# Attention maxima and sums cross the partition quadrants on VectorE instead of through a TensorE product

## Chip, cores, metric

The kernel runs on one core of one Trainium2 chip. The metric is device time in microseconds (us) of one execution, as the median of several runs.

## The reference

One transformer block with adaptive layer norm, float32 throughout. Cut to what matters here, the attention:

```python
h = _layernorm(x) * (1 + ca) + sa              # x: 2048 x 576
q = (h @ wq)                                   # 32 heads of 128
k, v = the last 512 cache rows of 16 key/value heads, each used by two query heads
scores = einsum("bhqd,bhkd->bhqk", q, k) * (128 ** -0.5)
p = softmax(scores, axis=-1)
o = einsum("bhqk,bhkd->bhqd", p, v)
x = x + ga * (o @ wo)
```

After it come a second layer norm and a gated MLP with 4608 hidden units. The softmax of one query runs over 512 keys: its maximum and its sum over the keys are what the change is about.

## The kernel before

Every float32 operand of a matmul is split into a high and a low fp32r part, and a product is made of three matmuls (high by high, low weight by high, high by low).

**Units.** The attention is cut into NU = 128 units: one head, one block of 512 queries, all 512 keys. A unit's scores lie transposed: keys on the 128 partitions, in four key tiles, and the 512 queries along the free dimension. So a maximum or a sum over the keys goes across partitions. `s_half` (twice per unit, 6 matmuls each, L495 to L497) makes the scores of two key tiles in a PSUM tile `s`.

**The maximum of a unit.** VectorE's transposing reduce (L500) takes 32x32 blocks of the scores, transposes each and reduces it: afterwards partition 32a+j holds, for key tile k and query block b, the maximum over the 32 keys of quadrant a (a quadrant is 32 partitions) for query 32b+j, in the tile `t4`, 128 x (4 x 16). `max_pre` reduces over the four key tiles (L508, into PSUM) and multiplies by a mask so that each quadrant's 16 numbers stand in a column group of their own, zero elsewhere (L509, into `t5`). `sum_pre` does the transposing reduce for the sums of the exponentials of the unit before (L515), into 16 more columns of `t5`. `spread` (L523) multiplies `t5`, 128 x 80, by the 0/1 matrix `quad`, which adds up the partitions that are equal modulo 32: every quadrant gets all four quadrants' maxima side by side, and the total of the sums. The profile shows it as two matmul records for each unit. `max_bc` then reduces the four column groups (L538), `sum_inv` takes the reciprocal of the sums (L528), and L551 transposes the maxima back into a 128x512 tile `mb`, which L568 subtracts from the scores, one half at a time. In the first four units and the last one (`by_pe`) the subtraction is a matmul instead.

**What follows in a unit.** ScalarE takes the exponential (L570) and its high part (L557), GpSimd the low part `lo` (L577, two halves). VectorE adds two of the four key tiles of exponentials (L583) and GpSimd the other two (L586) to get `ks`, which L515 reduces in the next unit. `pv_half` (L610 to L612) multiplies with the values one unit later, L533 and L618 multiply by the reciprocal sums, L622 and L626 split the result, and `wo_piece` (L637) projects pairs of units, two to four units later.

**What sets the order.** Each engine runs its instructions in the order in which the code writes them: a loop over the units writes them in steps, and at fixed times `run(u, k)` writes pieces of other work in between, from a list sorted by hand: casts and splits of weights, gates (L222), the layer norm, and towards the end preparations for the MLP (L851, L873). Within a unit PE's order is: scores (12 matmuls), query projection of the next unit (`qproj`, L423, 14), `spread`, a piece of the output projection (12 of 288 columns), the values product of the unit before (12), another output piece (12). A `psM` pool with two PSUM buffers of tag `mm` serves the query projections, the spread tiles `qm` and the value products in turn. DMAs are issued mainly from SP.

Of the kernel before, what the change touches and what calls it, by code (L numbers as in the profile page):

```python
# [7 lines left out]
F32 = mybir.dt.float32  # L8
F32R = mybir.dt.float32r
I32 = mybir.dt.int32  # L10
# [23 lines left out]
def kernel(  # L34
# [41 lines left out]

    ones = cp.tile([P, P], F32, name="ones")
    nc.vector.memset(ones, 1.0)

    ints = bp.tile([P, P], I32, tag="bc", name="ints")  # L80
    quad = cp.tile([P, P], F32, name="quad")
    nc.gpsimd.iota(ints, pattern=[[1, P]], base=P, channel_multiplier=-1)
    nc.vector.tensor_scalar(ints, ints, 31, None, op0=ALU.bitwise_and)
    nc.vector.tensor_scalar(quad, ints, 0.0, None, op0=ALU.is_equal)
    inta = bp.tile([P, 4], I32, tag="bc", name="inta")
    mask = cp.tile([P, 4], F32, name="mask")
    nc.gpsimd.iota(inta, pattern=[[-32, 4]], base=0, channel_multiplier=1)
    nc.vector.tensor_scalar(inta, inta, 5, None, op0=ALU.arith_shift_right)
    nc.vector.tensor_scalar(mask, inta, 0.0, None, op0=ALU.is_equal)

    intc = bp.tile([P, P], I32, tag="bc", name="intc")
    minus = cp.tile([P, P], F32R, name="minus")
# [386 lines left out]
        nc.vector.scalar_tensor_tensor(qlo[u], qst.pop(u)[0], SCALE, qhi[u].bitcast(F32),  # L479
                                       op0=ALU.mult, op1=ALU.subtract)  # L480

    st_, t4, t5, pt, hi_, lo_, bc, rb, rinv, ks_, pvps, done, o, bps = ({} for _ in range(14))

    def by_pe(u):
        return u < PE0 or u >= NU - PE1

    def s_half(u, h):
        g, qb, hd = unit(u)
        k = ks[g]
        t = psS.tile([P, 2, 512], F32, tag="s", name=f"s{u}_{h}")  # L490
        st_[u, h] = t
        for j in range(2):
            kt = 2 * h + j
            ps = t[:, j, :]
            nc.tensor.matmul(ps, k[:, kt, :], qhi[u], start=True, stop=False)  # L495
            nc.tensor.matmul(ps, k[:, 4 + kt, :], qhi[u], start=False, stop=False)  # L496
            nc.tensor.matmul(ps, k[:, kt, :], qlo[u], start=False, stop=True)  # L497
        if h == 0:
            t4[u] = sp.tile([P, 4, 16], F32, tag="t4", name=f"t4_{u}", bufs=1)
        nc.vector.tensor_reduce(t4[u][:, 2 * h:2 * h + 2, :].rearrange("p k b -> p (k b)"),  # L500
                                t.rearrange("p k (b j) -> p (k b) j", j=32),
                                axis=AX.X, op=ALU.max, apply_transpose=True)

    def max_pre(u):
        t5[u] = sp.tile([P, 5, 16], F32, tag="t5", name=f"t5_{u}", bufs=1)
        bps[u] = psM.tile([P, 512], F32, tag="mm", name=f"qm{u}")
        t = bps[u][:, 128:144]
        nc.vector.tensor_reduce(t, t4.pop(u).rearrange("p k b -> p b k"), axis=AX.X, op=ALU.max)  # L508
        nc.vector.tensor_tensor(t5[u][:, 0:4, :], mask[:, :, None].to_broadcast([P, 4, 16]),  # L509
                                t[:, None, :].to_broadcast([P, 4, 16]), op=ALU.mult)  # L510

    def sum_pre(u):
        if u + 1 == NU:
            t5[NU] = sp.tile([P, 5, 16], F32, tag="t5", name=f"t5_{NU}", bufs=1)
        nc.vector.tensor_reduce(t5[u + 1][:, 4, :],  # L515
                                ks_.pop(u).rearrange("p (b j) -> p b j", j=32),
                                axis=AX.X, op=ALU.add, apply_transpose=True)

    def spread(u):
        a, b = (0 if u < NU else 4), (5 if u else 4)  # L520
        if u == NU:
            bps[u] = psM.tile([P, 512], F32, tag="mm", name=f"qm{u}")
        nc.tensor.matmul(bps[u][:, a * 16:b * 16], quad,  # L523
                         t5.pop(u)[:, a:b, :].rearrange("p a b -> p (a b)"), start=True, stop=True)

    def sum_inv(u):
        r = rinv[u] = sp.tile([P, 16], F32, tag="ri", name=f"ri{u}", bufs=1)
        nc.vector.reciprocal(r, bps[u + 1][:, 64:80])  # L528

    def sum_bc(u):  # L530
        r = rinv.pop(u)
        rb[u] = bp.tile([P, 512], F32, tag="bc", name=f"rb{u}")
        nc.vector.transpose(rb[u].rearrange("p (b j) -> p b j", j=32),  # L533
                            r[:, :, None].to_broadcast([P, 16, 32]))

    def max_bc(u):
        r = bps[u][:, 256:272] if by_pe(u) else sp.tile([P, 16], F32, tag="r", name=f"r{u}", bufs=1)
        nc.vector.tensor_reduce(r, bps[u][:, :64].rearrange("p (a b) -> p b a", a=4), axis=AX.X, op=ALU.max)  # L538
# [986 lines left out]
    mlp = mlp_slots()  # L1525

    def last_unit():
        spread(NU)
        sum_inv(NU - 1)
        sum_bc(NU - 1)  # L1530
        o_mul(NU - 1)

# [80 lines left out]
    for u in range(NU):  # L1613
# [114 lines left out]
```

## Time and profile before

| | |
|---|---|
| median of 3 runs | 2887.05 us (2883.12 to 2887.52) |
| the profiled execution | 2884.48 us, its span 2882.7 us |
| granted TensorE clock, mean | 0.997 |
| attention units | from 35 to 1634 us of the span |
| MLP | from 1634 us to the end |

"Busy" is the time in which an engine runs at least one instruction. A row of a timeline view gives start, length, engine, line, operation, tiles, shapes and count; in square brackets stands how long the engine was idle before it and who ended that. A row of the groups view gives the count, then busy time and mean duration in ns, then the engine's idle time ahead of the group.

### The profile page before, as it was taken

What the parts mean: (1) busy time and instruction counts of PE and PEld (TensorE: products, weight loads), DVE (VectorE), ACT (ScalarE), POOL (GpSimd) and SP (SyncE); (2) the same over time, 40 slices, a digit from 0 to 9 for tenths busy, and PEclk for the clock granted to TensorE, in tenths of its full rate; (3) what the DMA queues carried; (4) which work ended last, traced back from release to release, by engine and by line L of the source; (5) the groups of instructions that cost most, each with busy time, mean ns of one, the idle gap of its engine ahead of it and who ended that gap; (6) DMA issues with size and microseconds to landing.
All of it is one profiled execution on the core that took longest, in us unless ns stands there. A gap on an engine that the chain in (4) does not pass through costs nothing.

```text
span 2882.7 us, 41271 instructions
## 1 busy us (share of the span) xinstructions
PE 2839.4 (98%) x15214; PEld 2476.9 (86%) x15214; DVE 2149.1 (75%) x2967; ACT 1496.2 (52%) x2105; POOL 2115.0 (73%) x1564
## 2 busy tenths in 40 slices
PE   6999999999999999999999999999999999999999
PEld 5788888888888888888888888888888888888888
DVE  7778788888878888777889756676677466666666
ACT  5666666666676666666656444444444222222221
POOL 5688888888888889776778666787787356656553
PEclk9999999999999999999999999999999999999999
DMA  4012222222223223322244456666667944444442
GB/s 161 23 46 70 72 101 83 71 90 99 97 83 100 92 64 135 103 71 87 66 131 145 149 216 218 233 243 232 228 228 256 354 160 156 154 154 155 160 153 106
DMA packets 164362, 399.59 MB, mean 139 GB/s; under 512 B 15040, under 2 KB 61888, under 8 KB 164160
## 3 DMA queue, kind: packets, MB, share of 16 engines
q1 hardware_dynamic: 132912, 284.84, 30.1%
q10 hardware_dynamic: 31248, 112.11, 9.9%
q8 instruction: 121, 1.98, 0.3%
q14 instruction: 81, 0.66, 0.1%
HBM read 271.16 MB, written 154.57 MB: 148 GB/s over the span
## 4 chain that ended last, share of the span: by engine, by line
PE 90%; POOL 3%; DVE 2%; ACT 2%; DMA 2%; issue 1%; SPq 0%; ACTq 0%; POOLq 0%; DVEq 0%
PE gu L981 26%; PE wo L637 13%; PE qps L423 13%; PE md L637 8%; PE st_P L1083 6%; PE s L497 4%; PE s L496 4%; PE s L495 4%; PE pv L612 4%; PE pv L611 4%; PE pv L610 4%; PE qm L523 1%; POOL lo L577 1%; ACT p L570 0%; DVE ws L788 0%
## 5 line engine op out<-in xcount | busy, mean ns | idle before, releaser
L577 POOL TENSOR_TENSOR lo<-p,hi 128x1024 fp32r<-128x1024 f32 x256 | 608.7, 2399 | 1.1 <-ACT hi L557 1.1
L586 POOL TENSOR_TENSOR ks<-ks,p 128x512 f32<-128x512 f32 x256 | 343.8, 1343 | 270.6 <-ACT p L570 212.6
L500 DVE TRANSPOSE_TENSOR_REDUCE t<-s 128x32 f32<-128x1024 f32 x256 | 316.6, 1244 | 136.9 <-PE s L497 125.6
L981 PE MATMUL gu<-hop_B,wop 128*128 128x512 f32 x1512 | 374.5, 391 | 0.2 <-DMA wop<-wk_P 0.2
L981 PEld LDWEIGHTS gu<-hop_B,wop 128*128 128x128 f32 x1512 | 275.0, 188 | 50.5 <-ACT lflh L966 0.9
L981 PE MATMUL gu<-hop_T,wop 128*128 128x512 f32 x1260 | 316.0, 391 | 0.0
L423 PE MATMUL qps<-hTa,wA 128*128 128x512 f32 x1288 | 311.4, 392 | 4.2 <-DVE hTa L371 2.1
L637 PE MATMUL wo<-woga,ohi 128*128 128x288 f32 x1472 | 306.5, 301 | 0.0
L568 DVE TENSOR_TENSOR p<-s,mb 128x1024 f32<-128x1024 f32 x246 | 290.2, 1218 | 4.1
L423 PEld LDWEIGHTS qps<-hTa,wA 128*128 128x128 f32 x1288 | 242.8, 189 | 57.4 <-DVE hTa L371 4.2
L557 ACT CAST hi<-p 128x1024 fp32r<-128x1024 f32 x256 | 269.1, 1051 | 7.1
L570 ACT ACTIVATE p<-p 128x1024 f32<-128x1024 f32 x246 | 259.8, 1056 | 7.6 <-DVE p L568 7.3
L637 PE MATMUL md<-wogb,hhi 128*128 128x288 f32 x1280 | 258.9, 295 | 3.6 <-DVE acc L648 2.6
L981 PEld LDWEIGHTS gu<-hop_T,wop 128*128 128x128 f32 x1260 | 227.8, 188 | 38.9
L475 ACT ACTIVATE qhi<-qps 128x512 fp32r<-128x512 f32 x128 | 76.5, 597 | 340.4 <-PE qps L423 340.4
L637 PEld LDWEIGHTS wo<-woga,ohi 128*128 128x128 f32 x1472 | 239.2, 189 | 7.3
L648 DVE TENSOR_TENSOR acc<-md,acc 128x576 f32<-128x576 f32 x160 | 120.7, 755 | 160.8 <-PE md L637 160.3
L637 PEld LDWEIGHTS md<-wogb,hhi 128*128 128x128 f32 x1280 | 212.2, 188 | 16.6 <-DVE acc L648 4.3
L637 PE MATMUL wo<-woga,olo 128*128 128x288 f32 x736 | 217.4, 295 | 0.3 <-POOL olo L626 0.2
L1092 DVE TENSOR_TENSOR acc<-st_P,acc 128x576 f32<-128x576 f32 x160 | 121.0, 757 | 128.0 <-PE st_P L1083 128.0
L637 PE MATMUL md<-wogb,hlo 128*128 128x288 f32 x640 | 188.6, 295 | 0.0
L646 ACT COPY acc<-wo 128x576 f32<-128x576 f32 x233 | 148.2, 636 | 66.8 <-PE wo L637 60.4
(274 smaller groups left out, 7107.2 us busy)
## 6 DMA issues: line engine op xcount, KB each, us to landing
wop<-wk_P SPq DMA_DIRECT2D x133, 640.0 KB
wk_P<-wop ACTq DMA_DIRECT2D x119, 640.0 KB
wr<-wlay SPq DMA_DIRECT2D x68, 384.0 KB
rogb<-wd SPq DMA_DIRECT2D x68, 288.0 KB
againq<-akq SPq DMA_DIRECT2D x18, 640.0 KB
rwA<-wq SPq DMA_DIRECT2D x32, 320.0 KB
wlay<-wg SPq DMA_DIRECT2D x36, 256.0 KB
roga<-wo SPq DMA_DIRECT2D x32, 288.0 KB
```

The source lines that it names most:

```text
L423: return [lambda i=i, a=a, b=b: nc.tensor.matmul(ps, a, b, start=(i == 0), stop=(i == n - 1)) for i, (a, b) in enumerate(ops)]
L500: nc.vector.tensor_reduce(t4[u][:, 2 * h:2 * h + 2, :].rearrange("p k b -> p (k b)"), t.rearrange("p k (b j) -> p (k b) j", j=32), axis=AX ...
L557: nc.scalar.copy(hi_[u, h], pt[u, h])
L568: nc.vector.tensor_tensor(p, t, bc[u][:, None, :].to_broadcast([P, 2, 512]), op=ALU.subtract)
L570: nc.scalar.activation(p, p, AF.Exp, bias=0.0, scale=1.0)
L577: nc.gpsimd.tensor_sub(lo_[u, h], pt[u, h], hi_[u, h].bitcast(F32))
L586: nc.gpsimd.tensor_tensor(ks_[u], ks_[u], p[:, j, :], op=ALU.add)
L637: nc.tensor.matmul(ps[:, half, :H2], a[:, sl], w[b][:, cs], start=(n == 0 and seed is None), stop=(n == 5), skip_group_check=seed is not None)
L646: nc.scalar.copy(av, ps[:, :, :H2])
L981: nc.tensor.matmul(ps, a, c, start=s not in heir(m) and i == 0 and s not in seeds_of(m), stop=i == len(ops) - 1, skip_group_check=True)
L1083: nc.tensor.matmul(ps[:, j, :H2], x[:, sl], w[:, y, :], start=n == 0 and not second, stop=n == 2, skip_group_check=True)
L1092: nc.vector.tensor_tensor(t, ps[:, :, :H2], t, op=ALU.add)
```

## The change

The maxima and sums no longer go through PE. The tile `t5` becomes 128 x 21 rows of 16 numbers. The transposing reduces write row 0 of a group of four rows for each key tile and for the sums; `cross` then moves with VectorE instructions whose output partitions differ from their input partitions (`move`: a reduce over an axis of length one). First partitions 64 to 127 to partitions 0 to 63 (5 x 16 numbers), then 32 to 63 to 0 to 31 (5 x 2 x 16). Then quadrant 0 holds everything: one reduce of 16 rows gives the maxima (256 numbers in), one of 4 rows gives the sums (64 in), and two more moves (32 numbers each) copy both to quadrant 1 and then to quadrants 2 and 3. `max_pre`, `spread` and `sum_inv` go, with the matrix `quad`, the mask and the PSUM tile `qm`; the reciprocal is taken in `sum_bc`. `max_bc` stands before the next unit's query projection in the code, where it stood behind it.

```diff
-        nc.vector.tensor_reduce(t4[u][:, 2 * h:2 * h + 2, :].rearrange("p k b -> p (k b)"),
+        nc.vector.tensor_reduce(t5[u][:, 8 * h:8 * h + 8:4, :],
                                 t.rearrange("p k (b j) -> p (k b) j", j=32),
                                 axis=AX.X, op=ALU.max, apply_transpose=True)
-    def max_pre(u):
-        t5[u] = sp.tile([P, 5, 16], F32, tag="t5", name=f"t5_{u}", bufs=1)
-        bps[u] = psM.tile([P, 512], F32, tag="mm", name=f"qm{u}")
-        t = bps[u][:, 128:144]
-        nc.vector.tensor_reduce(t, t4.pop(u).rearrange("p k b -> p b k"), axis=AX.X, op=ALU.max)
-        nc.vector.tensor_tensor(t5[u][:, 0:4, :], mask[:, :, None].to_broadcast([P, 4, 16]),
-                                t[:, None, :].to_broadcast([P, 4, 16]), op=ALU.mult)
-
-    def spread(u):
...
-        nc.tensor.matmul(bps[u][:, a * 16:b * 16], quad,
-                         t5.pop(u)[:, a:b, :].rearrange("p a b -> p (a b)"), start=True, stop=True)
-
-    def sum_inv(u):
-        r = rinv[u] = sp.tile([P, 16], F32, tag="ri", name=f"ri{u}", bufs=1)
-        nc.vector.reciprocal(r, bps[u + 1][:, 64:80])
+    def move(dst, src):
+        nc.vector.tensor_reduce(dst, src[..., None], axis=AX.X, op=ALU.max)
+
+    def cross(u):
+        t = t5.pop(u)
+        v = t[:, 0:20, :].rearrange("p (k a) b -> p k a b", a=4)[:, (0 if u < NU else 4):(5 if u else 4)]
+        move(v[0:64, :, 1, :], v[64:128, :, 0, :])
+        move(v[0:32, :, 2:4, :], v[32:64, :, 0:2, :])
+        r = rr_[u] = t[:, 15:21:5, :]
+        if u < NU:
+            nc.vector.tensor_reduce(r[0:32, 1, :], t[0:32, 0:16, :].rearrange("p n b -> p b n"), axis=AX.X, op=ALU.max)
+        if u:
+            nc.vector.tensor_reduce(r[0:32, 0, :], t[0:32, 16:20, :].rearrange("p n b -> p b n"), axis=AX.X, op=ALU.add)
+        w = slice(0 if u else 1, 2 if u < NU else 1)
+        move(r[32:64, w, :], r[0:32, w, :])
+        move(r[64:128, w, :], r[0:64, w, :])
 
     def sum_bc(u):
-        r = rinv.pop(u)
+        r = rr_.pop(u + 1)[:, 0, :]
+        nc.vector.reciprocal(r, r)
         rb[u] = bp.tile([P, 512], F32, tag="bc", name=f"rb{u}")
...
     def max_bc(u):
-        r = bps[u][:, 256:272] if by_pe(u) else sp.tile([P, 16], F32, tag="r", name=f"r{u}", bufs=1)
-        nc.vector.tensor_reduce(r, bps[u][:, :64].rearrange("p (a b) -> p b a", a=4), axis=AX.X, op=ALU.max)
-        if u:
-            sum_inv(u - 1)
+        r = rr_[u][:, 1, :]
...
         s_half(u, 0)
         s_half(u, 1)
         run(u, .5)
-        max_pre(u)
         if u:
             sum_pre(u - 1)
+        cross(u)
+        max_bc(u)
         run(u, 1)
         if u + 1 < NU:
             qproj(u + 1, 0, 14)
...
         run(u, 2)
-        spread(u)
-        max_bc(u)
         if u + 1 < NU:
             q_hi(u + 1)
```

VectorE's instructions in a middle unit (unit 78), from behind the two score reduces, before the change:

```order
L508 TENSOR_REDUCE qm_10576<-t_78_10565 128x16
L509 TENSOR_TENSOR t_78_10575<-mask,qm_10576 128x64
L515 TENSOR_REDUCE t_78_10575<-ks_10512 128x16
L538 TENSOR_REDUCE r_10596<-qm_10576 128x16
L528 RECIPROCAL ri_10598<-qm_10576 128x16
L551 STREAM_TRANSPOSE mb_10600<-r_10596 128x512
L568 TENSOR_TENSOR p_0_10633<-s_0_10558,mb_10600 128x1024
L568 TENSOR_TENSOR p_1_10638<-s_1_10567,mb_10600 128x1024
L533 STREAM_TRANSPOSE rb_10641<-ri_10598 128x512
```

And in the changed kernel, the next unit, at the same place (its line numbers are smaller; L501 is `move`, L510 and L512 the two reduces of `cross`, L536 the transpose of the maxima, L519 the reciprocal):

```order
L496 TENSOR_REDUCE t_79_10526<-ks_10481 128x16
L501 TENSOR_REDUCE t_79_10526<-t_79_10526 64x5x16
L501 TENSOR_REDUCE t_79_10526<-t_79_10526 32x5x32
L510 TENSOR_REDUCE t_79_10526<-t_79_10526 32x16
L512 TENSOR_REDUCE t_79_10526<-t_79_10526 32x16
L501 TENSOR_REDUCE t_79_10526<-t_79_10526 32x2x16
L501 TENSOR_REDUCE t_79_10526<-t_79_10526 64x2x16
L536 STREAM_TRANSPOSE mb_10543<-t_79_10526 128x512
L553 TENSOR_TENSOR p_0_10589<-s_0_10519,mb_10543 128x1024
L553 TENSOR_TENSOR p_1_10594<-s_1_10528,mb_10543 128x1024
L519 RECIPROCAL t_79_10526<-t_79_10526 128x16
L521 STREAM_TRANSPOSE rb_10598<-t_79_10526 128x512
```

Three instructions (L508, L509, L538) went, six came, and the reciprocal moved behind the two subtractions. Each of the six waits for the one ahead of it.

PE at the end of a query projection in unit 78, before the change (`qps` is the projection, `wo` an output piece):

```order
L423 MATMUL qps_10580<-hTa_6_1254,wA_9625 128x512
L423 MATMUL qps_10580<-hTa_7_1256,wA_9625 128x512
L523 MATMUL qm_10576<-t_78_10575,quad 128x80
L637 MATMUL wo_1_10544<-woga_9911,ohi_10298 128x288 x2
L637 MATMUL wo_1_10544<-woga_9911,olo_10300 128x288
```

And in the changed kernel, one unit later:

```order
L412 MATMUL qps_10545<-hTa_6_533,wA_10260 128x512
L412 MATMUL qps_10545<-hTa_7_535,wA_10260 128x512
L622 MATMUL wo_3_10511<-woga_9759,ohi_10140 128x288 x2
L622 MATMUL wo_3_10511<-woga_9759,olo_10142 128x288
L622 MATMUL wo_3_10511<-woga_10071,ohi_10323 128x288 x2
```

The product with `quad` is gone and PE goes from the projection straight to the output piece.

More of the change, by code (lines that the diff above doesn't have):

```diff
@@ L78 @@
     nc.vector.memset(ones, 1.0)
[L80 to L89, printed above, removed]
     intc = bp.tile([P, P], I32, tag="bc", name="intc")
@@ L480, in q_lo @@
                                        op0=ALU.mult, op1=ALU.subtract)
-    st_, t4, t5, pt, hi_, lo_, bc, rb, rinv, ks_, pvps, done, o, bps = ({} for _ in range(14))
+    st_, t5, pt, hi_, lo_, bc, rb, rr_, ks_, pvps, done, o = ({} for _ in range(12))
     def by_pe(u):
@@ L498, in s_half @@
         if h == 0:
-            t4[u] = sp.tile([P, 4, 16], F32, tag="t4", name=f"t4_{u}", bufs=1)
-        nc.vector.tensor_reduce(t4[u][:, 2 * h:2 * h + 2, :].rearrange("p k b -> p (k b)"),
+            t5[u] = sp.tile([P, 21, 16], F32, tag="t5", name=f"t5_{u}", bufs=1)
+        nc.vector.tensor_reduce(t5[u][:, 8 * h:8 * h + 8:4, :],
                                 t.rearrange("p k (b j) -> p (k b) j", j=32),
                                 axis=AX.X, op=ALU.max, apply_transpose=True)
-    def max_pre(u):
-        t5[u] = sp.tile([P, 5, 16], F32, tag="t5", name=f"t5_{u}", bufs=1)
-        bps[u] = psM.tile([P, 512], F32, tag="mm", name=f"qm{u}")
-        t = bps[u][:, 128:144]
-        nc.vector.tensor_reduce(t, t4.pop(u).rearrange("p k b -> p b k"), axis=AX.X, op=ALU.max)
-        nc.vector.tensor_tensor(t5[u][:, 0:4, :], mask[:, :, None].to_broadcast([P, 4, 16]),
-                                t[:, None, :].to_broadcast([P, 4, 16]), op=ALU.mult)
@@ L512, in sum_pre @@
     def sum_pre(u):
         if u + 1 == NU:
-            t5[NU] = sp.tile([P, 5, 16], F32, tag="t5", name=f"t5_{NU}", bufs=1)
-        nc.vector.tensor_reduce(t5[u + 1][:, 4, :],
+            t5[NU] = sp.tile([P, 21, 16], F32, tag="t5", name=f"t5_{NU}", bufs=1)
+        nc.vector.tensor_reduce(t5[u + 1][:, 16, :],
                                 ks_.pop(u).rearrange("p (b j) -> p b j", j=32),
                                 axis=AX.X, op=ALU.add, apply_transpose=True)
-    def spread(u):
[L520 to L523, printed above, removed]
-                         t5.pop(u)[:, a:b, :].rearrange("p a b -> p (a b)"), start=True, stop=True)
@@ L1527, in last_unit @@
     def last_unit():
-        spread(NU)
-        sum_inv(NU - 1)
+        cross(NU)
         sum_bc(NU - 1)
```

## The prediction, made before the changed kernel ran

> **What bounds the kernel now.** First the page: busy times, and the chain of work that ended last.
>
> ```profile
> PE 2839.4 (98%) x15214; PEld 2476.9 (86%) x15214; DVE 2149.1 (75%) x2967; ACT 1496.2 (52%) x2105; POOL 2115.0 (73%) x1564
> PE 90%; POOL 3%; DVE 2%; ACT 2%; DMA 2%; issue 1%; SPq 0%; ACTq 0%; POOLq 0%; DVEq 0%
> ```
>
> PE is the bound, and DVE's 75% is a mean over the attention and an MLP that the change doesn't touch. So I read a middle unit in the timeline: DVE's rows from one unit's scores to the next, and PE's rows around the two places where an output piece follows a 512-column product.
>
> ```profile
> 1005.13 2.61 DVE L500 TRANSPOSE_TENSOR_REDUCE t<-s 128x32 f32<-128x1024 f32 x2 [1.60 <-PE s L497]
> ...
> 1006.29 3.34 PE L423 MATMUL qps<-hTa,wA 128*128 128x512 f32 x14
> ...
> 1007.77 0.27 DVE L508 TENSOR_REDUCE qm<-t 128x16 f32<-128x64 f32 x1
> 1008.08 0.22 DVE L509 TENSOR_TENSOR t<-mask,qm 128x64 f32<-128x64 f32 x1
> 1008.22 0.70 DVE L515 TRANSPOSE_TENSOR_REDUCE t<-ks 128x16 f32<-128x512 f32 x1
> ...
> 1009.47 0.35 PE L523 MATMUL qm<-t,quad 128*128 128x80 f32 x2
> ...
> 1009.85 0.23 DVE L538 TENSOR_REDUCE r<-qm 128x16 f32<-128x64 f32 x1 [0.93 <-PE qm L523]
> ...
> 1010.00 0.25 DVE L528 RECIPROCAL ri<-qm 128x16 f32<-128x16 f32 x1
> ...
> 1010.16 0.67 DVE L551 STREAM_TRANSPOSE mb<-r 128x512 f32<-128x512 f32 x1
> ...
> 1011.30 0.39 PE L610 MATMUL pv<-hi,kv 128*128 128x512 f32 x1
> ...
> 1013.13 0.70 DVE L533 STREAM_TRANSPOSE rb<-ri 128x512 f32<-128x512 f32 x1
> ...
> 1013.76 0.65 DVE L479 SCALAR_TENSOR_TENSOR qlo<-qps,qhi 128x512 fp32r<-128x512 f32 x1
> ...
> 1013.82 0.39 PE L612 MATMUL pv<-lo,kv 128*128 128x512 f32 x1
> ...
> 1015.63 0.39 PE L495 MATMUL s<-qhi,kv 128*128 128x512 f32 x1
> ...
> 1016.08 0.40 PE L497 MATMUL s<-qlo,kv 128*128 128x512 f32 x1
> ...
> 1017.21 2.61 DVE L500 TRANSPOSE_TENSOR_REDUCE t<-s 128x32 f32<-128x1024 f32 x2 [1.17 <-PE s L497]
> ```
>
> The unit takes 1017.21 - 1005.13 = 12.08 us. PE has no gap; DVE waits twice, 0.93 us for `qm` and 1.17 us for scores. How much of such waiting there is shows in the groups of L500 and L538, asked for four stretches: units 0 to 5 (35 to 130 us), 6 to 108 (to 1380), ten units beside the second layer norm (to 1510), the last eight (to 1604).
>
> ```profile
> L500 DVE TRANSPOSE_TENSOR_REDUCE t<-s 128x32 f32<-128x1024 f32 x14 | 17.0, 1235 | 2.4 <-PE s L497 2.1
> ...
> L538 DVE TENSOR_REDUCE qm<-qm 128x16 f32<-128x64 f32 x4 | 0.9, 233 | 3.3 <-PE qm L523 3.3
> ...
> L538 DVE TENSOR_REDUCE r<-qm 128x16 f32<-128x64 f32 x2 | 0.4, 224 | 1.5 <-PE qm L523 1.5
> ```
> ```profile
> L500 DVE TRANSPOSE_TENSOR_REDUCE t<-s 128x32 f32<-128x1024 f32 x205 | 254.8, 1246 | 128.8 <-PE s L497 118.6
> L538 DVE TENSOR_REDUCE r<-qm 128x16 f32<-128x64 f32 x103 | 23.1, 224 | 91.9 <-PE qm L523 91.9
> ```
> ```profile
> L500 DVE TRANSPOSE_TENSOR_REDUCE t<-s 128x32 f32<-128x1024 f32 x22 | 27.0, 1238 | 4.7 <-PE s L497 3.9
> L538 DVE TENSOR_REDUCE r<-qm 128x16 f32<-128x64 f32 x10 | 2.2, 225 | 10.7 <-PE qm L523 10.7
> ```
> ```profile
> L500 DVE TRANSPOSE_TENSOR_REDUCE t<-s 128x32 f32<-128x1024 f32 x15 | 17.9, 1221 | 1.1 <-PE s L497 1.0
> L538 DVE TENSOR_REDUCE r<-qm 128x16 f32<-128x64 f32 x8 | 1.8, 224 | 4.9 <-PE qm L523 4.9
> ```
>
> DVE's free time is 118.6 + 91.9 = 210.5 us in the long stretch, 2.0 us for each unit, but 14.6 us in the next ten units and 5.9 us in the last eight (0.7 each). There DVE is as full as PE.
>
> **What goes on PE.** After the projection's last product (end 1006.29 + 3.34 = 1009.63) with `qm` and twelve output matmuls behind it, the next product starts at 1011.30, 1.67 us later; after L612 (end 1014.21), with twelve output matmuls alone, at 1015.63, 1.42 us later. The product with `quad` thus costs PE 0.25 us per unit, although its two records last 0.35. A unit bounded by PE goes from 12.08 to 11.83 us.
>
> **What comes on DVE.** The score reduce takes 1.246 us for 1024 numbers and L515 0.70 for 512: 1.07 ns for each and 0.16 fixed. L538 (64 numbers, from PSUM, 0.224) fits that. The two first moves (80 and 160 numbers a partition) would take 0.24 and 0.33, the last two (32 each) 0.19 each. The reduces over rows step 16 numbers at every read, as L508 does, and L508, with L538's shape, takes 0.27: 0.05 more. So the sum reduce (64 numbers) takes 0.23 to 0.28, the maximum (256) 0.43, or, if the 0.05 grows with the count, 0.63. The six together, X, take 1.61 to 1.86. I take 1.85, for the step is the only difference between L508 and L538 besides which memory they read and write. [...]
>
> No row shows an output in another quadrant than its input. From below this costs nothing, since half the partitions or all take the same time where the shapes are alike. From above I allow each of the four moves one more fixed part, 0.16: X = 2.5. I take nothing extra. [...]
>
> Each of the six, and L551, waits for the one ahead; such hand-overs take 0.03 us (L508 ends at 1008.04, L509 starts at 1008.08). From the end of the score reduces (1007.74) to L551 the DVE's own time was 1010.16 - 1007.74 - 0.93 = 1.49 us. Now it is L515 (0.70, overlapping by 0.08 what is ahead, as it does behind L509: end 1008.30, start 1008.22), X, and seven hand-overs (0.24): 0.86 + X = 2.71. So L551 starts 0.29 later after the scores than before, though it waits for nothing on PE. The reciprocal now stands before L533, 0.25 + 0.03 on its own. DVE's load per unit grows by 2.71 - 1.49 + 0.28 = **1.5 us** (1.26 at X = 1.61, 2.15 at X = 2.5).
>
> **What is late next.** `qlo` for the next unit (L479) ended at 1014.41, PE's first use is at 1016.08: 1.67 us of slack, of which 0.29 + 0.28 + 0.25 go. 0.85 is left: a plain unit is fine, and one late by less than that too. The tighter path is the GpSimd one: scores, L551, exponential, `ks`, then `lo`, which PE needs in the next unit. Where GpSimd also splits a query weight ahead of it, it reads:
>
> ```profile
> 1018.62 1.56 POOL L182 TENSOR_TENSOR wA<-rwA,wA 128x640 fp32r<-128x640 f32 x1
> 1020.14 4.76 POOL L577 TENSOR_TENSOR lo<-p,hi 128x1024 fp32r<-128x1024 f32 x2
> ```
> ```profile
> 1025.22 0.39 PE L612 MATMUL pv<-lo,kv 128*128 128x512 f32 x1
> ```
> ```profile
> L182 POOL TENSOR_TENSOR wA<-rwA,wA 128x640 fp32r<-128x640 f32 x29 | 45.7, 1575 | 0.0
> ```
>
> The second half of `lo` ends at 1024.90, PE wants it at 1025.22: 0.32 us. Two `quad` products lie between, so PE arrives 0.50 earlier, and `lo` ends 0.29 later: PE waits 0.47. There are 29 such splits in the long stretch; in 22 units, counted in the timeline, `lo` ends within 0.45 us of its use, most at 0.32 or 0.33. 22 x 0.47 = 10.3 us.
>
> **The sum**, against the profiled execution (2884.48 us, 2.6 below the median of the runs).
> - Long stretch: 103 x 0.25 = 25.8 us gained; 10.3 go back to `lo`. DVE's 210.5 us free pay for 103 x 1.5 = 155 and the 25.8, but L500 waited for scores 89 times only (the row below, from L500 asked alone in this stretch): 14 of the 103 units began with no wait, for gates and other work on DVE. They become 12.08 - 0.93 + 1.5 = 12.65 us of DVE, 0.8 more than PE's 11.83. The slack covers `qlo`, not `lo`; I charge 0.5 each, 7 us. Net 8.5 gained.
>
> ```profile
>   PE s L497: 118.6, 89
> ```
>
> - Next ten units: 10 x 1.5 = 15 us against 14.6 free: nothing gained.
> - Last eight units: 12 against 5.9; 6.1 us longer, less the 0.85 that `qlo` covers: 5 lost.
> - First six: PE isn't the bound there; 6 x 1.5 = 9 on DVE against 2.1 plus 4.8 us of waits: 2 lost.
> - PE's own waits for what DVE put into `qm` go, 3.2 us:
>
> ```profile
> PE qm L523 <- DVE t L515: 3.2, 4, 1.5
> ```
>
> 8.5 - 5 - 2 + 3.2 = 4.7 us gained, 0.16%: 2879.8 on the profiled execution, 2882.4 on the median. A part of DVE's load that I can't count, dependent instructions that start late in units that are late already, speaks for a little more, and I take **2884**. With X from 1.61 to 2.0 (0.1 us of X moves the sum by about 4 us: 22 times on `lo`, 14 + 8 + 6 times on DVE) the sum goes from 14 gained to 1 lost; charging the 14 uneven units their whole 0.8 and as much again for those behind them takes it to 10 lost. On the median the case is 2873 to 2897. As cover: the product that goes was PE time in full, and what comes is hidden behind PE only where DVE waited.
>
> **The rivals.**
> 1. *Nearly the whole gain.* The six cost at most 1.3 us, say because handed-over small instructions overlap more than their records show. Then 0.95 comes per unit, L551 starts 0.26 earlier than now, `lo`'s deficit shrinks to nothing, the last eight lose 1.7: 25.8 + 3.2 - 1.7 - 2 and up to 7 for uneven units, 18 to 25 gained: 2862 to 2873 with the edge of the forecast. For it: 2.0 us of free DVE time per unit in the long stretch. Against it: L538, the shortest reduce in the rows above, takes 0.22, and six of those are 1.3.
> 2. *DVE becomes the bound* (the other side). If the moves cost a fixed part more, X = 2.5 and 2.15 come per unit: 221 us in the long stretch against 210.5 - 25.8 free. It decides from (210.5 - 25.8) / 103 = 1.8 per unit, X = 2.15. At 2.15: 11 longer there by mean load, some 5 for unevenness, 7 in the next ten, 11 in the last eight, 6 in the first, and 3.2 back: 37 longer. At X = 2.2 the 4 us per 0.1 give some 10. 2898 to 2925. For it: the last eight units already have no room, as this one shows:
>
> ```profile
> 1549.38 0.22 DVE L538 TENSOR_REDUCE r<-qm 128x16 f32<-128x64 f32 x1 [0.54 <-PE qm L523]
> ...
> 1555.65 1.78 DVE L851 TENSOR_TENSOR h<-h,h 128x512 f32<-128x512 f32 x1
> 1557.35 2.37 DVE L500 TRANSPOSE_TENSOR_REDUCE t<-s 128x32 f32<-128x1024 f32 x2
> ```
>
> DVE there starts the scores late, with 0.54 us free in a whole unit, and a 512-number sum takes 1.78 instead of the 0.70 of L515's 512. If later starts bring more of these long ones, the price rises too. Against it: nothing shows that a move costs more than its numbers.
> 3. *It doesn't do what it says.* PE would gain nothing if weight loads and not products set its pace there. The two 1.67 and 1.42 us stretches speak against it. Without the 25.8, and with `lo` late by almost nothing, the 5, the 2 and a little for uneven units stay: 5 to 8 us longer, 2892 to 2895. [...]
>
> **How the numbers follow.** The forecast case (2873 to 2897) has a chance of 0.53, rival 1 0.20, rival 2 0.25, rival 3 0.02. About 0.2% (5.8 us) is what a measurement of this kernel can tell from no change. Of the forecast case 0.15 lies below 2881.3, 0.22 between, 0.16 above 2892.8. Faster: 0.20 + 0.15 = 0.35; the same 0.22; slower 0.25 + 0.16 + 0.02 = 0.43. The range reaches into both rivals, 2864 to 2913.
>
> **What would show it.** In the changed profile: (a) no L523, and plain units of 11.83 us; (b) the six at 0.24, 0.33, 0.63, 0.28, 0.19, 0.19 us; the maximum reduce is the one I know least; (c) the wait before L500 down from 1.17 to about 0.3 to 0.4 in plain units, no other wait ahead of the transpose; (d) waits of PE for `lo`, 22 or more, near 0.5 us each; (e) the last eight units longer than before, some by 0.7 us. The prediction is wrong if X is under 1.3 or over 2.1, if PE waits for `qlo` in the long stretch, or if the MLP's time moves.

## The result and the profile after

The changed kernel takes 2897.34 us (median of 6 runs, 2896.66 to 2899.86), the kernel before 2886.45 us (6 runs, 2883.12 to 2887.71). The ratio is 1.0043, with a 95% interval of 1.0033 to 1.0052: 0.4% slower, where a gain of about 0.1% was forecast. The profiled execution has a span of 2894.9 us (2882.7 before), 12.2 longer.

The page of the changed kernel, busy times and the chain that ended last:

```profile
PE 2825.1 (98%) x14956; PEld 2443.7 (84%) x14956; DVE 2302.0 (80%) x3351; ACT 1498.9 (52%) x2105; POOL 2125.3 (73%) x1562
PE 64%; DVE 10%; POOL 5%; issue 3%; ACT 2%; DMA 2%; ACTq 0%; POOLq 0%; SPq 0%; DVEq 0%
```

PE is busy for 14.3 us less, yet its part of the chain fell from 90% to 64% and DVE's rose from 2% to 10%. A middle unit of the changed kernel, DVE's rows from one unit's scores to the next:

```profile
1253.81 2.61 DVE L489 TRANSPOSE_TENSOR_REDUCE t<-s 128x32 f32<-128x1024 f32 x2 [0.87 <-PE s L486]
1256.34 0.67 DVE L496 TRANSPOSE_TENSOR_REDUCE t<-ks 128x16 f32<-128x512 f32 x1
1257.04 0.57 DVE L501 TENSOR_REDUCE t<-t 64x80 f32<-64x80 f32 x2
1257.65 0.59 DVE L510 TENSOR_REDUCE t<-t 32x16 f32<-32x256 f32 x1
1258.27 0.25 DVE L512 TENSOR_REDUCE t<-t 32x16 f32<-32x64 f32 x1
1258.56 0.39 DVE L501 TENSOR_REDUCE t<-t 32x32 f32<-32x32 f32 x2
1258.98 0.71 DVE L536 STREAM_TRANSPOSE mb<-t 128x512 f32<-128x512 f32 x1
...
1265.63 1.25 DVE L489 TRANSPOSE_TENSOR_REDUCE t<-s 128x32 f32<-128x1024 f32 x1 [0.87 <-PE s L486]
```

The unit takes 1265.63 - 1253.81 = 11.82 us, and the only wait left is the one for scores. So the plain unit went from 12.08 to 11.83 as forecast; 48 of the 103 units from 6 to 108 take this, from first score to first score. The durations of the six, and the waits for scores, over units 6 to 108 (groups, forms apart, 127 to 1372 us):

```profile
L489 DVE TRANSPOSE_TENSOR_REDUCE t<-s 128x32 f32<-128x1024 f32 x206 | 253.1, 1240 | 63.1 <-PE s L486 55.1
L510 DVE TENSOR_REDUCE t<-t 32x16 f32<-32x256 f32 x103 | 60.7, 589 | 3.6
```

The first two moves take 0.231 and 0.307 us, the sum reduce 0.253, the last two moves 0.176 and 0.180; with 0.589 for the maximum, X is 1.74 (1.85 was taken).

Where the time went shows when the span is cut at the first score product of units 0, 6, 109, 119 and 127 and at the first `gu` product of the MLP (all from the timelines; us; the kernels below the second row are the experiments):

| kernel | units 0-5 | 6-108 | 109-118 | 119-126 | last unit to MLP | MLP to the end |
|---|---|---|---|---|---|---|
| before | 91.1 | 1253.5 | 126.6 | 97.1 | 11.7 | 1267.3 |
| changed | 91.9 | 1244.5 | 132.5 | 104.3 | 17.8 | 1268.4 |
| late_ten | 91.9 | 1244.3 | 126.4 | 104.4 | 17.8 | 1270.6 |
| last9_pe | 92.5 | 1243.8 | 132.6 | 97.2 | 11.7 | 1273.7 |
| last1_pe | 92.6 | 1243.3 | 132.5 | 104.3 | 15.5 | 1270.8 |
| from109_pe | 91.8 | 1244.1 | 126.6 | 97.0 | 11.7 | 1274.2 |
| no_cross | 86.5 | 1232.6 | 123.5 | 95.5 | 12.4 | 1270.5 |
| max2 | 94.3 | 1272.4 | 140.8 | 109.3 | 18.3 | 1267.5 |
| pre | 90.0 | 1237.7 | 129.0 | 101.0 | 16.4 | 1267.8 |
| pre_from109_pe | 90.2 | 1237.3 | 126.3 | 97.1 | 11.7 | 1275.3 |
| pre_late_ten | 90.5 | 1237.4 | 124.5 | 101.0 | 17.0 | 1267.5 |
| pre_late_ten_last9 | 90.9 | 1237.4 | 124.6 | 97.0 | 11.7 | 1268.5 |
| warm | 92.0 | 1244.8 | 132.6 | 104.3 | 16.1 | 1271.0 |

From the first row to the second the attention changes by +0.8, -9.0, +5.9, +7.2 and +6.1 us, and the MLP by +1.1. The long stretch gained nearly what the prediction said; the three places behind it took back 19.2 us.

**The ten units.** DVE and PE in one of the four units where the layer norm's affine step stands (L340 before, L329 now). First before the change, DVE's rows, then PE's output piece behind the product with `quad`:

```profile
1447.17 0.70 DVE L515 TRANSPOSE_TENSOR_REDUCE t<-ks 128x16 f32<-128x512 f32 x1
1447.80 0.77 DVE L340 TENSOR_SCALAR lfb<-ltb,mcol,mcol 128x512 f32<-128x512 f32 x1
1449.69 0.22 DVE L538 TENSOR_REDUCE r<-qm 128x16 f32<-128x64 f32 x1 [1.12 <-PE qm L523]
```
```profile
1449.31 0.35 PE L523 MATMUL qm<-t,quad 128*128 128x80 f32 x2
1449.45 0.52 PE L637 MATMUL wo<-againo,ohi 128*128 128x288 f32 x2
```

The same place in the changed kernel, and who waited for L329 in units 109 to 118:

```profile
1443.33 0.39 DVE L501 TENSOR_REDUCE t<-t 32x32 f32<-32x32 f32 x2
1443.76 0.71 DVE L536 STREAM_TRANSPOSE mb<-t 128x512 f32<-128x512 f32 x1
1444.39 0.77 DVE L329 TENSOR_SCALAR lfb<-ltb,mcol,mcol 128x512 f32<-128x512 f32 x1
```
```profile
1445.21 0.54 PE L622 MATMUL wo<-againo,ohi 128*128 128x288 f32 x2 [1.23 <-DVE lfb L329]
```
```profile
  PE wo L622: 5.0, 4
```

Before, L340 ran inside the wait for `qm`, which cost nothing. Now the code writes it behind the whole crossing and the transpose. It reads a PSUM tile of the pool `psW`, and the next output piece needs that buffer: PE stands still for 1.23 us, four times, 5.0 us.

**The last unit.** It has no next projection that covers its maxima. Windows of the changed kernel from its first score product on (columns: stretch, its length, busy time and count of each engine, granted clock of TensorE, share and rate of DMA):

```profile
1608.70:1617.40 8.70, 6.82 (x34) 4.98 (x33) 8.67 (x11) 4.90 (x6) 5.77 (x4) 1.00 0.30 90
1617.40:1622.00 4.60, 1.71 (x6) 0.83 (x6) 3.74 (x12) 0.91 (x2) 2.26 (x1) 0.88 0.53 174
1622.00:1626.50 4.50, 4.50 (x16) 4.11 (x17) 1.74 (x3) 4.12 (x6) 1.60 (x2) 0.50 0.05 15
1626.50:1630.00 3.50, 3.50 (x18) 3.05 (x18) 0.76 (x1) 1.20 (x2) 3.42 (x3) 0.82 0.00 0
```

And its DVE rows:

```profile
1613.32 1.77 DVE L836 TENSOR_TENSOR h<-h,h 128x512 f32<-128x512 f32 x1
1615.01 2.37 DVE L489 TRANSPOSE_TENSOR_REDUCE t<-s 128x32 f32<-128x1024 f32 x2
...
1620.34 0.71 DVE L531 STREAM_TRANSPOSE mb<-rr 128x512 f32<-128x512 f32 x1
```

DVE is busy without a break (8.67 of 8.70 us) and reaches the last scores at 1615.01, behind a backlog of the units ahead; the maxima come at 1620.34. PE runs for only 1.71 of the 4.60 us up to 1622, and then its granted clock is 0.50 for 4.5 us and 0.82 on the mean of another 3.5. At the same place before the change the four subtractions came 8.8 us after the first score product (1612.47), PE was busy for 3.27 of 4.40 us, and the clock stayed at 1.00:

```profile
1608.00:1612.40 4.40, 3.27 (x16) 2.25 (x14) 2.81 (x9) 0.60 (x2) 3.83 (x2) 1.00 0.77 264
1612.40:1616.00 3.60, 3.60 (x20) 2.92 (x20) 2.27 (x4) 3.57 (x6) 1.29 (x1) 1.00 0.38 112
```

The four subtractions, before and with the change:

```profile
1612.47 1.20 PE L564 MATMUL s<-mr,minus 128*128 128x512 f32 x4
```
```profile
1621.76 2.07 PE L549 MATMUL s<-mr,minus 128*128 128x512 f32 x4 [1.31 <-ACT mr L534]
```

They start 13.1 us after the unit's first score product (1608.7) instead of 8.8, which is 4.3 of the 6.1 us. From their start to the first `gu` product it is 4.75 us instead of 2.94, with no wait in between: 1.8 us for the low clock.

### The profile page after: what moved, and what is told of

It is laid out like the page before. It is cut to its first block, busy times and chain, and to the rows that moved or that the text cites. A ratio compares the mean times of both kernels' runs of the same rounds, so it can differ in the third digit from the quotient of the medians.

```text
span 2894.9 us, 41010 instructions
## 1 busy us (share of the span) xinstructions
PE 2825.1 (98%) x14956; PEld 2443.7 (84%) x14956; DVE 2302.0 (80%) x3351; ACT 1498.9 (52%) x2105; POOL 2125.3 (73%) x1562
## 4 chain that ended last, share of the span: by engine, by line
PE 64%; DVE 10%; POOL 5%; issue 3%; ACT 2%; DMA 2%; ACTq 0%; POOLq 0%; SPq 0%; DVEq 0%
PE gu L966 24%; PE wo L622 7%; PE md L622 7%; PE qps L412 7%; PE st_P L1068 6%; PE s L486 2%; PE s L485 2%; PE s L484 2%; PE pv L597 2%; DVE t L489 2%; PE pv L596 2%; PE pv L595 2%; POOL lo L562 2%; DVE p L553 1%; DVE t L501 1%
## 5 line engine op out<-in xcount | busy, mean ns | idle before, releaser
L571 POOL TENSOR_TENSOR ks<-ks,p 128x512 f32<-128x512 f32 x256 | 349.8, 1366 | 268.1 <-ACT p L555 168.0
L489 DVE TRANSPOSE_TENSOR_REDUCE t<-s 128x32 f32<-128x1024 f32 x256 | 313.2, 1237 | 67.7 <-PE s L486 58.7
L622 PE MATMUL wo<-woga,ohi 128*128 128x288 f32 x1472 | 299.8, 295 | 2.3 <-POOL woga L171 1.4
L622 PEld LDWEIGHTS wo<-woga,ohi 128*128 128x128 f32 x1472 | 246.2, 188 | 19.6 <-POOL woga L171 4.3
L966 PE MATMUL gu<-hy_T,wop 128*128 128x512 f32 x540 | 174.7, 392 | 0.5 <-POOL wop L745 0.5
```

The lines of the kernel that those rows point to most:

```text
L489: nc.vector.tensor_reduce(t5[u][:, 8 * h:8 * h + 8:4, :], t.rearrange("p k (b j) -> p (k b) j", j=32), axis=AX.X, op=ALU.max, apply_transp ...
L571: nc.gpsimd.tensor_tensor(ks_[u], ks_[u], p[:, j, :], op=ALU.add)
L622: nc.tensor.matmul(ps[:, half, :H2], a[:, sl], w[b][:, cs], start=(n == 0 and seed is None), stop=(n == 5), skip_group_check=seed is not None)
L966: nc.tensor.matmul(ps, a, c, start=s not in heir(m) and i == 0 and s not in seeds_of(m), stop=i == len(ops) - 1, skip_group_check=True)
```

## The experiments

Three theories stood at the start. *Order*: the ten units lose because L329 moved behind the crossing. *Backlog*: the last eight units push DVE behind, and the last unit pays for it, with the lowered clock on top. *Load*, the rival to both: DVE has 1.4 us more per unit, and where it stands doesn't matter. All times are medians; ratios are to the kernel before, run on the same chip (17 to 26 runs of it beside the first eight, 9 beside the last three).

### late_ten: the crossing behind the inserted work, units 109 to 118

```diff
             sum_pre(u - 1)
-        cross(u)
-        max_bc(u)
+        if not (109 <= u < 119):
+            cross(u)
+            max_bc(u)
         run(u, 1)
...
         run(u, 2)
+        if 109 <= u < 119:
+            cross(u)
+            max_bc(u)
```

> The changed kernel, with the crossing and the transpose of the maxima written behind the inserted work (after run(u, 2)) in units 109 to 118 only. Order theory: the ten units lost 5.9 us because the affine step of the layer norm (L329, about 1.25 us), which stood in the wait for qm before the change, now stands behind the crossing, so that the output pieces wait for their PSUM buffer. Then units 109 to 118 take 126.6 to 128 us from first score to first score instead of 132.5, and the run is 4 to 6 us faster than the changed kernel (2891 to 2893). Load theory: DVE has 1.5 us more work per unit in ten units that had 14.6 us free, and its place doesn't matter: 131.5 to 133.5 us, no change of the run (2896 to 2898). Both expect the last nine units to stay as they are in the changed kernel.

2892.6 us, ratio 1.0022 (1.0013 to 1.0031). Units 109 to 118 take 126.4 us instead of 132.5, and the last nine units are as in the changed kernel. DVE's rows of the same unit:

```profile
1439.35 0.67 DVE L496 TRANSPOSE_TENSOR_REDUCE t<-ks 128x16 f32<-128x512 f32 x1
1439.94 0.77 DVE L329 TENSOR_SCALAR lfb<-ltb,mcol,mcol 128x512 f32<-128x512 f32 x1
1440.74 0.57 DVE L501 TENSOR_REDUCE t<-t 64x80 f32<-64x80 f32 x2
```

L329, which takes 0.77 us and not the 1.25 expected, is back behind the sum reduce, and nobody waits for it. The work on DVE is the same to the instruction, so load alone is not the cause there: order is.

### last9_pe, last1_pe, from109_pe: the TensorE product back from a unit on

`old(u)` is `u >= 119`, `u >= 127` or `u >= 109`; for those units `max_pre`, `spread` and `sum_inv` are those of before, on rows of the same tile, with `quad` brought by a DMA into the tile of ones that is no longer needed.

```diff
+        if old(u):
+            max_pre(u)
         if u:
             sum_pre(u - 1)
-        cross(u)
-        max_bc(u)
+        if not old(u):
+            cross(u)
+            max_bc(u)
...
         run(u, 2)
+        if old(u):
+            spread(u)
+            max_bc(u)
```

> The changed kernel, with the TensorE product of before in units 119 to 127 and for the last sums (quad comes back by a DMA into the tile of ones, three units ahead). Backlog theory: the eight units let DVE fall behind, and the last unit inherits that, whose late maxima leave PE idle for about 4 us, after which its clock is halved. Then all of it comes back: 5.6 us in units 119 to 125, 1.5 in unit 126, 6 between the last scores and the first product of the MLP, 1.6 at the low clock; 13 to 15 us faster than the changed kernel, 2882 to 2885. Own-chain theory: the six instructions in the last unit are themselves the longer chain; then the same comes back here, and only the next run tells them apart.

2885.8 us, ratio 1.0005 (0.9997 to 1.0014), 11.5 us faster than the changed kernel, a little less than the 13 to 15 expected. Units 119 to 126 and the last unit go back to 97.2 and 11.7 us, their times before the change.

> The changed kernel, with the TensorE product of before in the last unit and for the last sums only. Backlog theory: the last unit's scores still find DVE behind by about 3 us, so at most 2 to 3 us come back, 2894 to 2897, and PE is still idle for 3 us or more ahead of the subtraction of the maxima, with a clock of 0.5 behind it. Own-chain theory: 6 to 8 us come back, 2889 to 2891, PE idle for under 2 us there and at full clock behind it.

2896.72 us, ratio 1.0038 (1.0024 to 1.0052): at most a microsecond. The last unit takes 15.5 us instead of 17.8. DVE still comes late:

```profile
1616.14 2.37 DVE L505 TRANSPOSE_TENSOR_REDUCE t<-s 128x32 f32<-128x1024 f32 x2
```

L505 starts 6.3 us after the unit's first score product (1609.8), L489 in the changed kernel 6.3 after it (1608.7), L500 before 2.2 after it (1605.92 against 1603.7). Of the 6.1 us that the last unit lost, 3.8 remain with the old chain (15.5 against 11.7): the backlog. The other 2.3 are not all the unit's own chain. The subtractions start here 12.6 us after the first score product, 0.5 sooner than the 13.1 of the changed kernel, and that is what the chain costs:

```profile
1622.44 1.20 PE L591 MATMUL s<-mr,minus 128*128 128x512 f32 x4 [0.87 <-ACT mr L576]
```

The rest, 1.8 us, is the low clock, which this run doesn't have. That was expected wrongly: the clock stayed at 1.00, with PE busy for 2.87 us of the same 4.60 and not for 1.71.

```profile
1617.40:1622.00 4.60, 2.87 (x12) 1.45 (x10) 3.63 (x9) 0.23 (x1) 3.39 (x2) 1.00 0.59 170
1622.00:1626.50 4.50, 4.05 (x21) 3.35 (x22) 2.67 (x4) 4.44 (x7) 1.33 (x2) 1.00 0.24 83
```

> The changed kernel in units 0 to 108, and the TensorE product of before from unit 109 on. If the three places add up as the positions in the two traces say, this keeps the 9 us gained by unit 109 and loses nothing behind it: 2876 to 2879, a ratio to the kernel before of 0.9965 to 0.9975. If the gain up to unit 109 is given back anywhere else (the MLP, the end of the attention), 2883 to 2888.

2881.31 us, ratio 0.9988 (0.9979 to 0.9997): 4 us faster than before, not 8 or 9. At the first `gu` product this kernel is 8.2 us ahead of before (1607.2 against 1615.4), as the three places add up. In its profile the MLP then takes 1274.2 us instead of 1267.3. What PE waited for there:

```profile
PE md L664 <- DVE acc L675: 6.2, 3, 3.6
```

The longest of these three, 3.6 us, stands behind a sum on DVE that took 7.27 us where its like takes 0.94 (last section). Over all profiles here the MLP takes 1267 to 1275 us, and its code is the same in all. The profile of `pre_from109_pe` below has the same wait of 3.6 us behind a sum of 7.30 and the longest MLP; no other profile has a sum on DVE over 6.1 us there. But the two profiled executions are 2.2 and 5.3 us above the medians of their kernels, so they may not stand for all runs. Whether the kernels that arrive at some times have the long MLP more often, or by chance, stays open.

### no_cross and max2: the price of the chain from both sides

```diff
     def cross(u):
-        t = t5.pop(u)
...
+        rr_[u] = t5.pop(u)[:, 12:17:4, :]
```
```diff
         if u < NU:
+            nc.vector.tensor_reduce(r[32:64, 1, :], t[0:32, 0:16, :].rearrange("p n b -> p b n"), axis=AX.X, op=ALU.max)
             nc.vector.tensor_reduce(r[0:32, 1, :], t[0:32, 0:16, :].rearrange("p n b -> p b n"), axis=AX.X, op=ALU.max)
```

> The changed kernel without the six crossing instructions: nothing crosses the quadrants, and the transposes read one row of the uncrossed maxima and sums. It leaves that part of the computation out, so its time is that of TensorE's gain alone. DVE theory (every loss of the changed kernel is DVE being late; TensorE would have gained 0.25 us in every unit): units 6 to 108 take 1226 to 1229 us from first score to first score (1253.5 before, 1244.5 with the change), the last eight 12.0 or less each, and PE is at full clock behind the last unit; 28 to 33 us faster than the kernel before, 2852 to 2857. Rival, PE theory (the uneven units are late for reasons on PE and GpSimd that have nothing to do with the six): the long stretch stays at 1235 us or more, 2862 or slower.

2857.18 us, ratio 0.9903 (0.9890 to 0.9915), 28.6 us faster than before. The long stretch takes 1232.6 us, between the two theories: TensorE's gain is there (it was 1253.5), but 14 us over 103 x 11.83 stay. The weight loads of PE waited for this (127 to 1372 us in the changed kernel, then 122 to 1355 us without the crossing):

```profile
PEld pv L597 <- POOL lo L562: 10.4, 23, 1.1
PEld wo L622 <- POOL olo L611: 5.5, 11, 0.8
PEld s L486 <- DVE qlo L468: 4.5, 5, 1.7
```
```profile
PEld pv L586 <- POOL lo L551: 7.3, 21, 1.1
PEld wo L611 <- POOL olo L600: 2.8, 4, 1.2
```

Of the 10.4 us for `lo`, 7.3 are there without a crossing, most of them as waits of 0.25 us: PE comes 0.25 us earlier with each product that goes, and the low part doesn't come earlier with the maxima. In one such unit the first half of the subtraction is done at some 990.8 us, but ScalarE takes its exponential only at 993.15, behind two copies of an output piece for which it had waited 1.04 us. The crossing's own part is the rest and the waits for `qlo`. So this run prices the product and the crossing together, and not the product alone: DVE has 0.4 us less per unit in it than in the kernel before (9.48 against 9.88 us busy in units 6 to 108).

> The changed kernel with the reduce of the maxima written twice, its first result into a place that is overwritten: 0.59 us more and a hand-over, 0.62 per unit, in the chain of DVE. The prediction's slope of 4 us for 0.1 us gives 25 us more, 2919 to 2925. Bound theory (DVE is now the bound, so a unit grows by all that is added): 126 x 0.62 = 78 us more, 2970 to 2976. Slack theory (plain units have 0.9 us of slack ahead of qlo, so they stay at 11.83 and only the units that are uneven already grow): 15 to 35 us more, with plain units of 11.83 to 11.9 still there.

2942.15 us, ratio 1.0199 (1.0186 to 1.0212): 45 us more than the changed kernel for 0.62 us per unit, 7.2 us for each 0.1. Not the 78 of a kernel bound by DVE throughout, and more than the 35 of the slack theory. In the long stretch it is 27.9 us (4.5 for 0.1), and 34 of its 103 units still take 11.8 (48 in the changed kernel); units 109 to 118 add 8.3, units 119 to 126 add 5.0. PE's loads wait for `qlo` 29 times now:

```profile
PEld pv L598 <- POOL lo L563: 20.1, 28, 1.1
PEld s L486 <- DVE qlo L468: 16.5, 29, 2.3
```

### pre: key tiles reduced first

All 128 partitions reduce their own four key tiles (as L508 did before the change), so that one row crosses and not four.

```diff
+        if u < NU:
+            nc.vector.tensor_reduce(t[:, 0, :], t[:, 10:14, :].rearrange("p n b -> p b n"), axis=AX.X, op=ALU.max)
-        v = t[:, 0:20, :].rearrange("p (k a) b -> p k a b", a=4)[:, (0 if u < NU else 4):(5 if u else 4)]
+        v = t[:, 0:8, :].rearrange("p (k a) b -> p k a b", a=4)[:, (0 if u < NU else 1):(2 if u else 1)]
...
-            nc.vector.tensor_reduce(r[0:32, 1, :], t[0:32, 0:16, :].rearrange("p n b -> p b n"), axis=AX.X, op=ALU.max)
+            nc.vector.tensor_reduce(r[0:32, 1, :], t[0:32, 0:4, :].rearrange("p n b -> p b n"), axis=AX.X, op=ALU.max)
```

> The changed kernel, the key tiles reduced first on all 128 partitions (64 numbers), so that the moves and the second reduce carry a quarter of the numbers: seven instructions of about 0.25, 0.18, 0.23, 0.25, 0.25, 0.18 and 0.18 us, 1.52 us against 1.74, and one hand-over more, 0.18 us less per unit. By the slope of 4 us for 0.1 us 7 us faster than the changed kernel, 2889 to 2891. If the number of handed-over instructions is what costs and not their length, no faster than the changed kernel, 2896 to 2899.

2883.35 us, ratio 0.9991 (0.9983 to 1.0000), 14 us faster than the changed kernel, twice what was expected. Its groups over units 6 to 108:

```profile
L501 DVE TENSOR_REDUCE t<-t 64x32 f32<-64x32 f32 x206 | 37.2, 180 | 7.1
L512 DVE TENSOR_REDUCE t<-t 32x16 f32<-32x64 f32 x103 | 26.2, 255 | 3.6
L514 DVE TENSOR_REDUCE t<-t 32x16 f32<-32x64 f32 x103 | 25.1, 244 | 0.0
L506 DVE TENSOR_REDUCE t<-t 128x16 f32<-128x64 f32 x103 | 23.0, 223 | 0.0
L501 DVE TENSOR_REDUCE t<-t 32x64 f32<-32x64 f32 x103 | 21.3, 207 | 3.6
L501 DVE TENSOR_REDUCE t<-t 32x32 f32<-32x32 f32 x103 | 18.1, 176 | 3.5
```

The seven take 2 x 0.180 + 0.255 + 0.244 + 0.223 + 0.207 + 0.176 = 1.47 us instead of 1.74; with one hand-over more the chain is 0.23 shorter. The first six units gain 1.9 us, the long stretch 6.8 (2.9 for 0.1), and the three places behind it 8.2 together: 3.5, 3.3 and 1.4. Against the kernel before, this version is at the edge of what can be told from no change.

### The versions that put it together

`pre_from109_pe` is this crossing up to unit 108 and the TensorE product behind it; `pre_late_ten` uses the shorter crossing in all units, in units 109 to 118 at the late place; `pre_late_ten_last9` is the same with the TensorE product from unit 119 on. Their edits are those above.

> The crossing of the run before (key tiles first) in units 0 to 108 and the TensorE product of before from unit 109 on. From the 4 us that the mixture with the plain crossing gained on the kernel before, and 5 to 6 us less in the long stretch: 2874 to 2877, a ratio to before of 0.996 to 0.9975. If length is not what costs, 2880 to 2882.

2870.01 us, ratio 0.9953 (0.9940 to 0.9966), 4 us under the range expected.

> The crossing with key tiles first in all units, and in units 109 to 118 written behind the inserted work: no TensorE product for the maxima anywhere. Units 109 to 118 took 129.0 us with the first and 126.4 with the second alone (132.5 in the changed kernel, 126.6 before). Order theory: the two add, since without a crossing at all they took 123.5: 124 to 126 us, 3 to 5 us faster than the shorter crossing alone, 2878 to 2880. If the place no longer matters once the chain is shorter, 129 us and 2882 to 2885.

2875.04 us, ratio 0.9967 (0.9954 to 0.9979). Units 109 to 118 take 124.5 us, the two edits add; the whole is 3 us under the range expected.

> The same up to unit 118, and the TensorE product of before in units 119 to 127 and for the last sums. The last eight units go back from 87.7 to 84.9 us and the end of the attention to what it was before the change (8 to 9 us less between unit 119 and the first product of the MLP): 2868 to 2871, within 2 us of the mixture that uses the product from unit 109 on, and the ten units in it 124 to 126 us against 126.3 there.

2868.82 us, ratio 0.9945 (0.9933 to 0.9958), the fastest here: 0.55% faster than the kernel before and 1% faster than the changed one. It can't be told apart from `pre_from109_pe`.

### warm: products in PE's idle time of the last unit

```diff
+                for i in range(6):
+                    nc.tensor.matmul(wt, ks[unit(u)[0]][:, i % 4, :], qhi[u], start=i == 0, stop=i == 9)
```

(after the second of the last unit's four products with `lo`; four more behind the last of them)

> The changed kernel with ten products of 512 columns in the last unit whose result nobody reads, six in the wait for the last low parts of unit 126 and four in the wait for the maxima, on PE where it is idle for 1.6 and 1.3 us. Clock theory: the products behind were slow because PE had been idle, so the granted clock stays at 1.00, the four subtractions take 0.23 us each instead of 0.43 and the twelve of the output piece 0.13 instead of 0.24, and the first product of the MLP comes 2 to 4 us earlier than in the changed kernel: 2893 to 2896. If the low clock has another cause, the clock is 0.5 again and the time 2897 to 2898.

2898.12 us, ratio 1.0045 (1.0030 to 1.0060): no difference in the time. In the profile the clock theory holds, the clock stays at 1.00 and the first `gu` product comes 16.1 us after the unit's first score product instead of 17.8, though the four subtractions start 13.1 us after it as in the changed kernel:

```profile
1617.40:1622.00 4.60, 4.36 (x18) 2.85 (x17) 4.29 (x12) 0.02 (x1) 3.15 (x2) 1.00 0.36 125
1622.00:1626.50 4.50, 4.11 (x22) 3.16 (x21) 2.68 (x5) 4.47 (x6) 1.29 (x1) 1.00 0.63 228
```

So the low clock costs 1.7 us up to that product, less than the 2 to 4 expected. They are lost again in the MLP, which takes 2.6 us longer in this profile; with the scatter of the MLP this can't be told from chance.

## Why the prediction was wrong

The forecast was a gain of some 3 us on the median, and 11 were lost. Its steps, in order:

- **Right: PE.** 0.25 us per unit: plain units take 11.83 us.
- **X: right, a little high, and in part by luck.** 1.74 against 1.85. The moves cost what their numbers cost (0.231, 0.307, 0.176, 0.180 against 0.24, 0.33, 0.19, 0.19), so writing to another quadrant added nothing here. That half the partitions take as long as all has its rows in the trace before: L371 takes 0.694 us on 64 partitions and 0.686 on 128, with 512 numbers on each. The maximum took 0.589 (0.63 taken), but the reason for 0.63 was misread: the code of L538 steps 16 numbers at every read too, so the step can't be what makes L508 slower, and in `pre` the same step on 64 numbers (L506) takes 0.223, no more than L538. Why 256 numbers take some 0.15 more than 256 x 1.07 ns and the fixed 0.16, no run here separates. Not foreseen: the transpose L536 takes 0.71 instead of 0.67.
- **Right: DVE's load; wrong: the wait that was to be left.** Ahead of the scores, 0.3 to 0.4 us was to be left in a plain unit, and 0.87 is there. The 1.17 that it started from was not that of a plain unit; the row at 1005.13 has 1.60, as have the units at 1199, 1211 and 1236 us (1.59 to 1.61). From 1.60 + 0.93 to 0.87, with the unit 0.26 shorter, DVE has 1.40 more per unit, near the 1.5 forecast. On the mean of the long stretch the wait fell from 118.6 / 103 = 1.15 to 55.1 / 103 = 0.53 us.
- **Nearly right: the long stretch.** 8.5 gained and 3.2 for `qm` were forecast, and 9.0 came. 22 units late on `lo` with 10.3 us were forecast, and 23 waits with 10.4 us are there; that the shift of 0.50 us on PE makes most of it, `no_cross` shows too. The waits for `qlo` (5, 4.5 us), which the forecast named as a sign of being wrong, are there as well.
- **Nearly right: the first six** (0.8 lost, 2 forecast) **and the last eight** (units 119 to 126: 7.2 lost, 5 forecast; part of it are sums that take longer than before, last section).
- **Failed: "Next ten units: 10 x 1.5 = 15 us against 14.6 free: nothing gained."** 5.9 were lost. The step weighed DVE's load against its free time and treated the moved `max_bc` as if only its own waits mattered. It left out what the move puts behind it: the work that the code writes between the old place and the new one (`run(u, 1)` and `run(u, 2)`), here the affine step, which holds a PSUM buffer of the output pieces. `late_ten` brings all of it back with the same load.
- **Failed: the end of the sum.** Nothing stood in it for the last unit, which has no projection to cover its maxima and inherits the backlog of the eight. It took 6.1 us: 3.8 from the backlog, 0.5 from the unit's own longer chain and 1.8 from the low clock (`last1_pe`, `warm`). `last9_pe` brings all of it back. Behind the first `gu` product the distance to the trace before grows from 11.1 to 11.7 us while the clock is still low, and by another 1.0 up to 1668 us at full clock; `warm`, whose clock never fell, has this last step too.
- **Too small outside the long stretch: the slope.** 4 us for 0.1 us of X; measured 6 (`pre`: 14 / 2.35) and 7.2 (`max2`). In the long stretch it is 2.9 and 4.5; most of the rest comes from units 109 to 126.

The rivals: DVE as the bound (2898 to 2925) came nearest in its time, but its reason, dearer moves, did not hold. Nearly the whole gain (rival 1) was to come at a chain of 1.3 us; at 1.47 (`pre`) it is 2 us. That PE gains nothing (rival 3) is out by the plain units of 11.83 us.

## What to carry to other kernels

A chain that moves from one engine to another also moves ahead of or behind everything the code writes between its old and its new place; list those instructions and ask for each who holds a buffer for whom. Mean free time of an engine over a stretch says nothing about the stretch's end: price the last unit by itself, with the lateness that the units ahead hand to it. And where two engines are both nearly full, give each stretch the form that suits it: here DVE takes the crossing where it waits, and TensorE where DVE doesn't.

## What the runs showed of the hardware

**The clock after broken idle time.** PE's granted clock halved in a stretch of 4.6 us in which PE ran for 1.71 us, with gaps of 1.58 and 1.31 us (windows of 1 us put the fall near 1621.0). It stayed at 1.00 where PE ran for 2.87 of 4.60 (`last1_pe`), for 3.27 of 4.40 (before) and, with the added products, for 4.36 of 4.60 us (`warm`). So here the clock fell with no single gap longer than 1.58 us; whether it is the length of one gap that counts or the idle time of the whole stretch, no run here separates.

**Long sums on DVE beside GpSimd.** A DVE instruction that reads two SBUF tiles took 7.27 us in the MLP of `from109_pe`, and the same shape 0.94 us right behind it. DVE's rows and GpSimd's at that place:

```profile
2137.78 7.27 DVE L815 TENSOR_TENSOR wr<-wr,wr 128x768 f32<-128x768 f32 x1
...
2146.23 0.94 DVE L815 TENSOR_TENSOR ws<-wr,wr 128x768 f32<-128x768 f32 x1
```
```profile
2138.41 1.28 POOL L787 TENSOR_TENSOR wop<-wr,wop 128x512 fp32r<-128x512 f32 x1
...
2144.20 1.97 POOL L849 TENSOR_TENSOR hx_T<-hx_T 128x512 f32<-128x512 f32 x1
```

From 2138.41 to 2146.17 GpSimd runs six two-input instructions without a gap (the first and the last of them stand above), and the DVE sum ends 0.85 us into L849, which itself takes 1.97 us where it took 1.29 at 2135.92. That the sum waited for these instructions is not shown: the rows only stand side by side, and no run here tests it. The same kind of row, L836 at 1.46 to 1.78 us, is part of the load of the last eight units: its eight `lfb` sums took 9.4 us together before the change (0.67 to 1.69 each) and take 12.6 with it (1.46 to 1.69). That GpSimd is what makes these long is not shown either.
